# Gated recurrence and gated causal unit: GpSimd's square, addition and product as one operation per chunk of 1024 tokens, under a newly written order of all queues

## Chip, cores, metric

The kernel runs on one core of a Trainium2 chip. The metric is the time of one execution on the device in microseconds (us). Three runs of the kernel before took 288.52, 288.65 and 288.95 us; the median is 288.65 us.

## What is computed

Four sequences of 6336 tokens with 256 channels, 25344 tokens in all. First a gated linear recurrence, then a gated unit with a causal convolution of five taps:

```python
sig_r, sig_i = sigmoid(r_gate), sigmoid(i_gate)
a = exp(8 * sig_r * log(sigmoid(a_param)))
u = sqrt(max(1 - a*a, 1e-6)) * sig_i * x
for t in range(S): h = a[:, t] * h + u[:, t]; y[:, t] = h      # h = 0 at t = 0
gate = sigmoid(sum_k conv_w[k] * y[:, t - 4 + k])              # zeros ahead of t = 0
out = (gate * (y @ w_val)) @ w_out
```

Inputs and output are float32. The kernel keeps most intermediate tiles in bfloat16.

## The kernel before

**Tiling.** The tokens are cut into 51 windows (w0 to w50): w0, w1 and the last have 256 tokens, all others 512. Windows are joined to 28 chunks (line 17): chunks 0 to 2 and 26, 27 hold one window, chunks 3 to 25 two, so chunk c holds w(2c-3) and w(2c-2), 1024 tokens. The 256 channels are two halves h of 128 partitions.

**Stations of a chunk.** Each word of the string ORDER (line 38) is one step, a two-letter name with its numbers, and behind @ the PSUM banks that it writes. The string is played word by word (line 557), each step issuing its instructions on one engine; so ORDER fixes the order within every engine's queue. Between engines only semaphores order the work. An engine never passes a waiting instruction.

- lr, li, lx (window): loads of r, i, x, 512 KB each, on SyncE's queue (L292), into rings of four windows each. A load waits until its place was read for the last time.
- ta, tb (chunk): ScalarE's tanh of half of r (L310) and of i (L313). They free the places of r and i.
- pp (window, L320): GpSimd adds one to the tanh of i, in place. up (window, L332): GpSimd multiplies it with x and writes u, freeing the place of x. For windows 1, 2 and 6 uv does both on VectorE (L346), from a copy of x that TensorE makes (xp, L337).
- tr (chunk, h): TensorE transposes the tanh of r, for one chunk or for a pair (GROUPS, line 35; L357). ex (chunk, h): ScalarE's exponential gives a (L378).
- sq (chunk, h, L386): GpSimd squares a into the ring of squares. In two places ScalarE does it (sa.25.1 and sa.27.1, L394).
- rt (batch, L405): ScalarE's square root of 1 - a*a for a batch of mostly three chunks (BATCHES, line 20; rt.10 is chunks 23 to 25, rt.11 is 26 and 27). The square root needs another activation table, so a table is loaded ahead of nearly every rt and another behind it (L562).
- nt (chunk): TensorE transposes the roots (L420); xg: VectorE multiplies them with u (L450); xt: TensorE transposes back (L461); sc (chunk, h): VectorE's scan, the recurrence itself (L483). For chunks 26 and 27 u is transposed first and the product follows (L435, L446).
- cv (window): TensorE's convolution with 20 matmuls (L495). tg: ScalarE's tanh of it (L502), into a ring of three. vl: y @ w_val (L510). gv: VectorE's product (L515). ou: the last product (L525). cd or ca: copy to SBUF by VectorE (L533) or ScalarE (L535). st: store on SyncE's queue (L546).
- wm: five matmuls whose result nobody reads (L364).

**What orders the work around the change.** GpSimd's queue holds only sq, pp, up and four casts at the start. A chunk of 1024 tokens takes six instructions there: two sq, two pp, two up, each over 128x1024 elements. rt of a batch waits for all squares of the batch, xg of a chunk for its u, and lx of a later window for up of the window that held its place.

Places in the rings: r and i use place (w + 1) mod 4, so that the two windows of a chunk stand side by side; x uses w mod 4, by which w3 (place 3) and w4 (place 0) do not.

Of the kernel before, what the change touches and what calls it, by code (L numbers as in the profile page):

```python
# [9 lines left out]
P = 128  # L10
# [3 lines left out]
ACT = mybir.ActivationFunctionType  # L14
# [3 lines left out]
    [512, 512], [512, 512], [512, 512], [512, 512], [512, 512], [512, 512], [512, 512], [512, 512], [512, 512],  # L18
    [512, 512], [512, 512], [512, 512], [512, 512], [512, 512], [512, 512], [512, 512], [512], [256]]
BATCHES = [[0], [1], [2], [3, 4], [5, 6, 7], [8, 9, 10], [11, 12, 13], [14, 15, 16], [17, 18, 19], [20, 21, 22],  # L20
    [23, 24, 25], [26, 27]]
# [17 lines left out]
s_ident s_small s_kt s_diag lr.2 lr.0 s_wl.3 lr.1 li.0 lr.3 s_wl.2 ta.2 ta.0 lr.4 tr.0.1@0 tr.2.0@1 lr.6 ta.1 lr.5  # L39
tr.1.0@2 tb.0 tr.0.0@3 li.1 tr.2.1@4 ex.2.0 li.2 tr.1.1@5 li.3 ex.1.1 lx.0 ex.0.1 sq.1.1 li.4 ex.1.0 sq.2.0 ex.0.0  # L40
ex.2.1 sq.1.0 ta.3 sq.2.1 pp.0 sq.0.0 sq.0.1 ta.4 tb.1 lr.10 tr.3.0@4,5 tb.2 lr.9 lr.8 lr.7 lx.2 tr.3.1@2,3 ex.3.0
s_wl.1 up.0 lx.1 lx.4 wm.10@6 ex.3.1 sq.3.0 wm.5@6 lx.3 wm.3@6 tb.3 sq.3.1 wm.9@6 wm.6@6 ta.6 pp.4 sq.4.1 ta.5 lr.13
li.5 xp.2@2,3 li.6 sq.4.0 li.7 lr.14 tr.5.0@4,5 lx.6 uv.2 pp.3 rt.0 rt.2 nt.0@0 up.4 xg.0 rt.1 xt.0@0,1 xp.1@2 rt.3
sc.0.0 nt.1@3 up.3 lx.5 nt.2@0 uv.1 s_wl.0 xg.1 xg.2 xt.1@2,3 sc.0.1 lx.7 sc.1.0 nt.3@6,7 lr.12 sc.1.1 xg.3 ex.5.0
xt.2@0,1 sc.2.1 sc.2.0 tb.4 cv.0@2,3 tr.5.1@4,5 xt.3@6,7 lr.11 li.8 sq.5.0 ex.5.1 tg.0 sc.3.0 pp.5 sc.3.1 cv.2@0,1
s_wcast cv.1@4,5 ta.8 xp.6@2,3 uv.6 vl.0@6,7 tg.1 tg.2 vl.2@0,1 up.5 ta.7 sq.6.1 lx.8 li.9 li.10 lr.17 lr.18
nt.4@2,3 gv.0 tb.5 tr.7.0@6,7 ou.0.0@4 gv.2 ex.7.0 xg.4 sq.6.0 cd.0.0 tr.7.1@0,1 sq.5.1 vl.1@2,3 ou.2.0@4,5 ex.7.1
gv.1 xt.4@6,7 ou.1.0@2 lx.9 li.12 cv.4@0,1 cd.2.0 cv.3@4,5 pp.7 sq.7.1 tb.6 pp.8 sq.7.0 tg.4 tg.3 rt.4 sc.4.1 st.0
sc.4.0 li.11 lr.15 lr.16 st.2 up.7 pp.9 li.14 li.13 vl.3@0,1 vl.4@4,5 gv.3 gv.4 cd.1.0 ou.3.0@0,1 pp.10 up.8 sq.8.1
cd.3.0 cv.6@6,7 st.1 ou.4.0@2,3 wm.12@4 tg.6 cd.4.0 wm.1@4 nt.5@2,3 xg.5 lx.10 tb.7 st.3 vl.6@0,1 gv.6 ta.9 xt.5@2,3  # L50
ou.6.0@0,1 cv.5@6,7 nt.6@4,5 ta.10 up.9 sc.5.0 sc.5.1 lx.11 up.10 wm.0@2 tr.9.0@2,3 tg.5 st.4 lx.12 tb.8 vl.5@6,7
ex.9.0 xg.6 cd.6.0 xt.6@4,5 pp.11 sq.8.0 pp.12 tr.9.1@0,1 up.11 ex.9.1 li.16 li.15 lr.19 lr.20 gv.5 lr.22 st.6 lr.21
nt.7@6,7 cv.7@2,3 sc.6.1 up.12 ou.5.0@0,1 sc.6.0 sq.9.0 tg.7 tb.9 cv.8@2,3 cd.5.0 xg.7 lx.13 lx.14 li.18 ta.11
vl.7@4,5 cv.9@0,1 xt.7@6,7 gv.7 tr.11.1@4 tg.9 tg.8 ex.11.1 ta.12 ou.7.0@0,1 st.5 lx.15 lx.16 li.17 li.19 lr.26
lr.24 sc.7.1 sc.7.0 cv.10@2,3 vl.10@4,5 wm.7@7 vl.8@6,7 tg.10 sq.10.1 pp.13 pp.14 sq.10.0 cd.7.0 sq.9.1 pp.15 gv.10
rt.5 gv.8 st.7 lr.23 li.20 vl.9@2,3 up.13 up.14 tr.12.0@0 pp.16 ou.10.0@4,5 gv.9 ou.8.0@6,7 cd.8.0 ou.9.0@2,3
wm.16@1 nt.8@6,7 tr.11.0@1 cd.9.0 cd.10.0 tb.10 sq.11.1 up.16 xg.8 cv.11@4,5 lx.17 st.9 lr.25 xt.8@6,7 sc.8.1 tg.11
vl.11@2,3 wm.17@4 ex.12.0 tr.12.1@0 nt.9@4,5 gv.11 pp.17 up.15 pp.18 ex.11.0 ex.12.1 sq.12.1 sq.11.0 cv.12@2,3
sq.12.0 xg.9 ta.13 wm.13@7 ou.11.0@4,5 sc.8.0 xt.9@0,1 cd.11.0 cv.14@6,7 cv.13@4,5 tb.11 tg.12 ta.14 tg.14 tg.13
tr.13.0@2,3 tr.13.1@6,7 sc.9.0 ex.13.0 sc.9.1 up.17 st.10 li.21 vl.12@4,5 ex.13.1 nt.10@0,1 lx.18 li.22 gv.12 up.18  # L60
xg.10 lr.28 st.8 lr.27 tb.12 vl.13@2,3 st.11 ou.12.0@4,5 xt.10@0,1 cv.16@6,7 pp.20 pp.19 sq.13.1 gv.13 ou.13.0@2,3
lx.20 lx.21 lr.30 lx.19 ta.15 sq.13.0 pp.21 up.20 cd.12.0 cv.15@4,5 sc.10.1 sc.10.0 lr.29 li.23 tg.16 cd.13.0 li.24
lx.22 tg.15 vl.16@6,7 vl.14@4,5 gv.14 cv.18@0,1 vl.15@2,3 pp.22 rt.6 up.19 li.25 ou.14.0@4,5 gv.16 gv.15 cd.14.0
wm.14@6 ou.15.0@2,3 tg.18 lr.31 li.26 nt.11@4,5 sq.14.0 sq.14.1 up.21 up.22 vl.18@6,7 cd.15.0 xg.11 xt.11@4,5 tb.13
gv.18 cv.17@0,1 nt.12@6,7 ta.16 lr.32 lx.23 sc.11.1 lx.24 st.15 pp.23 pp.24 xg.12 st.13 li.27 li.28 vl.17@2,3
tr.15.1@6,7 sc.11.0 tg.17 tb.14 up.23 ou.16.0@0,1 cd.16.0 ex.15.1 ta.17 cv.19@4,5 lr.34 lr.33 tg.19 gv.17 xt.12@0,1
tr.15.0@6,7 st.14 lx.25 sc.12.0 sc.12.1 li.30 ou.17.0@2,3 pp.25 ex.15.0 ou.18.0@4,5 cv.20@6,7 up.24 tb.15 cd.17.0
cd.18.0 tg.20 cv.21@0,1 pp.26 sq.15.1 sq.16.1 nt.13@2,3 vl.19@6,7 tg.21 xg.13 st.12 lx.26 lx.28 st.17 lx.27 sq.15.0
li.29 st.16 li.31 lr.35 gv.19 vl.20@0,1 gv.20 xt.13@2,3 ou.20.0@0,1 sc.13.0 sq.16.0 vl.21@6,7 ou.19.0@4,5 gv.21
ta.18 cd.20.0 sc.13.1 ou.21.0@6,7 cv.22@0,1 lr.38 st.20 lr.36 rt.7 ca.19.0 li.32 lr.37 up.25 pp.27 up.26 pp.28 lx.29  # L70
nt.14@4,5 cd.21.0 xg.14 vl.22@2,3 tr.17.1@6,7 tg.22 tb.16 up.28 up.27 ex.17.1 nt.15@0,1 lx.30 gv.22 xg.15 xt.14@4,5
tr.17.0@2,3 cv.23@0,1 sc.14.0 sc.14.1 ex.17.0 pp.30 cv.24@6,7 pp.29 st.19 tg.23 vl.24@2,3 ou.22.0@0,1 tg.24 gv.24
vl.23@6,7 xt.15@4,5 ta.19 sq.18.1 sq.18.0 sq.17.0 sq.17.1 ou.24.0@2,3 tb.17 cd.22.0 gv.23 li.33 li.34 cv.26@0,1
up.29 cd.24.0 ou.23.0@6,7 st.18 ta.20 pp.32 ca.23.0 tg.26 cv.25@2,3 up.30 pp.31 sc.15.0 tg.25 li.35 tr.19.0@6,7
nt.16@0,1 vl.25@2,3 sc.15.1 xg.16 st.21 cv.27@4,5 ex.19.0 gv.25 lx.31 lx.33 xt.16@0,1 st.22 lx.32 lx.34 tr.19.1@6,7
lr.40 li.36 lr.39 st.23 tb.18 sc.16.0 sc.16.1 ou.25.0@2,3 tg.27 sq.19.0 ex.19.1 cv.28@4,5 tg.28 pp.34 sq.20.0
vl.28@6,7 vl.26@4,5 sq.19.1 lr.42 lr.41 cd.25.0 gv.28 wm.19@0 vl.27@2,3 gv.26 up.31 ou.28.0@6,7 up.32 up.34 pp.33
# [29 lines left out]
def kernel(  # L107
# [82 lines left out]
    with tc.manual_schedule():  # L190
# [403 lines left out]
```

## Time and profile before

| | |
|---|---|
| runs | 288.52, 288.65, 288.95 us |
| span of the profiled execution, first to last instruction | 286.4 us |
| from that span to the median of the runs | 2.25 us |
| ScalarE (ACT) busy | 273.6 us, 198 instructions |
| TensorE (PE) busy | 251.8 us |
| VectorE (DVE) busy | 246.8 us |
| GpSimd (POOL) busy | 241.6 us, 161 instructions |
| moved by DMA | 104.76 MB, mean 366 GB/s |

The profiled execution's own time is known by its span only; what lies around the span is taken as the 2.25 us to the median. The page of the profile names busy time by engine, then 40 slices of the span with the busy share in tenths (9 is 90% or more), and the groups of instructions with their mean duration. The view by form keeps shapes apart; the waits say which engine stood still for whom; the timeline and the chain of waits give start and length in us. Instructions of one engine overlap a little at their ends, so the step from one start to the next is shorter than a duration, and busy time by windows joins the overlaps.

### The profile page before, as it was taken

What the parts mean: (1) busy time and instruction counts of PE and PEld (TensorE: products, weight loads), DVE (VectorE), ACT (ScalarE), POOL (GpSimd) and SP (SyncE); (2) the same over time, 40 slices, a digit from 0 to 9 for tenths busy, and PEclk for the clock granted to TensorE, in tenths of its full rate; (3) what the DMA queues carried; (4) which work ended last, traced back from release to release, by engine and by line L of the source; (5) the groups of instructions that cost most, each with busy time, mean ns of one, the idle gap of its engine ahead of it and who ended that gap; (6) DMA issues with size and microseconds to landing.
All of it is one profiled execution on the core that took longest, in us unless ns stands there. A gap on an engine that the chain in (4) does not pass through costs nothing.

```text
span 286.4 us, 6382 instructions
## 1 busy us (share of the span) xinstructions
PE 251.8 (88%) x2552; PEld 171.1 (60%) x2576; DVE 246.8 (86%) x214; ACT 273.6 (96%) x198; POOL 241.6 (84%) x161
## 2 busy tenths in 40 slices
PE   1387778899999999988988999989989899999993
PEld 1253447456656767455756676656646774767562
DVE  4002898969999899999999999999999999999991
ACT  5999999999999999999999999999999999898984
POOL 1659589899999999999999999999996999874600
PEclk9999999999999999999999999999999999999999
DMA  7999999999999999999999999999999999994536
GB/s 243 384 373 407 409 403 408 388 366 376 410 408 366 418 367 392 414 410 334 405 364 413 411 332 356 420 416 419 415 401 333 359 416 406 364 356 170 192 150 256
DMA packets 29996, 104.76 MB, mean 366 GB/s; under 512 B 3335, under 2 KB 3854, under 8 KB 29966
## 3 DMA queue, kind: packets, MB, share of 16 engines
q1 hardware_dynamic: 29952, 104.35, 94.5%
q8 instruction: 20, 0.33, 0.5%
q14 instruction: 10, 0.08, 0.1%
q10 hardware_dynamic: 14, 0.01, 0.0%
HBM read 78.39 MB, written 25.95 MB: 364 GB/s over the span
## 4 chain that ended last, share of the span: by engine, by line
ACT 33%; PE 29%; DVE 14%; issue 12%; DMA 8%; SPq 1%; ACTq 0%; DVEq 0%
ACT ering L405 8%; PE banks L495 8%; DVE yring L483 7%; PE banks L525 7%; DMA rring<-in_r_gate_dram 6%; ACT tgring L502 6%; ACT taring L310 5%; ACT tbring L313 5%; ACT aring L378 5%; PE banks L510 5%; PE banks L461 3%; DVE tgring L515 3%; PE banks L420 3%; ACT L562 3%; DVE oring L533 2%
## 5 line engine op out<-in xcount | busy, mean ns | idle before, releaser
L386 POOL TENSOR_TENSOR ering<-aring 128x1024 f32<-128x1024 f32 (+2 forms) x54 | 91.5, 1714 | 16.7 <-ACT aring L378 16.4
L332 POOL TENSOR_TENSOR uring<-tbring,xring 128x1024 bf16<-128x1024 bf16 (+1 forms) x48 | 101.1, 2119 | 3.6 <-DMA xring<-in_x_dram 3.1
L483 DVE TENSOR_TENSOR_SCAN yring<-aring,yring,banks 128x1024 bf16<-128x1024 f32 (+5 forms) x50 | 101.7, 2064 | 2.1 <-PE banks L461 1.9
L495 PE MATMUL banks<-yring,diag 64*64 64x512 bf16 (+7 forms) x1080 | 62.1, 361 | 2.3 <-ACT aring L378 1.6
L515 DVE SCALAR_TENSOR_TENSOR tgring<-tgring,banks 128x1024 bf16<-128x1024 bf16 (+1 forms) x51 | 59.1, 1178 | 4.0 <-PE banks L510 3.4
L320 POOL TENSOR_SCALAR tbring<-tbring 128x1024 bf16<-128x1024 bf16 (+1 forms) x48 | 49.1, 1032 | 6.8 <-ACT tbring L313 6.7
L378 ACT ACTIVATE aring<-banks,khf 128x2048 f32<-128x2048 bf16 (+3 forms) x38 | 54.2, 1476 | 0.4 <-PE banks L357 0.3
L525 PE MATMUL banks<-wo,tgring 128*128 128x256 bf16 x396 | 51.0, 274 | 3.7 <-DVE tgring L515 3.2
L502 ACT ACTIVATE tgring<-banks 128x1024 bf16<-128x1024 f32 (+1 forms) x51 | 50.2, 1011 | 2.0 <-PE banks L495 1.9
L510 PE MATMUL banks<-yring,wv 128*128 128x512 bf16 (+4 forms) x192 | 48.1, 359 | 3.7 <-ACT tgring L502 1.9
L310 ACT ACTIVATE taring<-rring 128x2048 bf16<-128x2048 f32 (+2 forms) x28 | 47.9, 1718 | 1.4 <-DMA rring<-in_r_gate_dram 1.4
L525 PEld LDWEIGHTS <-tgring 128*128 128x128 bf16 x396 | 41.2, 114 | 13.1 <-DVE tgring L515 8.8
L313 ACT ACTIVATE tbring<-iring 128x2048 bf16<-128x2048 f32 (+2 forms) x28 | 48.2, 1726 | 0.0
L405 ACT ACTIVATE ering<-ering 128x4096 bf16<-128x4096 f32 (+5 forms) x16 | 44.8, 2840 | 0.1
L495 PEld LDWEIGHTS <-diag 64*64 64x64 bf16 x1080 | 29.0, 106 | 25.6 <-issue 9.9
L533 DVE COPY oring<-banks 128x1024 f32<-128x1024 f32 (+1 forms) x36 | 41.9, 1182 | 1.4 <-PE banks L525 0.7
L357 PE MATMUL banks<-ident_b,taring 128*128 128x128 bf16 x396 | 29.9, 230 | 9.4 <-ACT taring L310 6.7
L357 PEld LDWEIGHTS <-taring 128*128 128x128 bf16 x396 | 26.5, 103 | 14.2 <-ACT taring L310 7.4
L510 PEld LDWEIGHTS <-wv 128*128 128x128 bf16 x216 | 19.7, 98 | 24.5 <-issue 10.3
L450 DVE TENSOR_TENSOR uring<-banks,uring 128x2048 bf16<-128x2048 bf16 (+2 forms) x26 | 29.4, 1134 | 3.5 <-PE banks L420 3.2
L420 PE MATMUL banks<-ident,ering 128*128 128x128 f32 x192 | 28.3, 289 | 1.1 <-ACT ering L405 0.9
L461 PE MATMUL banks<-ident,uring 128*128 128x128 f32 x192 | 25.9, 276 | 3.5 <-DVE uring L450 2.8
(49 smaller groups left out, 154.0 us busy)
## 6 DMA issues: line engine op xcount, KB each, us to landing
rring<-in_r_gate_dram SPq DMA_DIRECT2D x48, 512.0 KB, 8.2
iring<-in_i_gate_dram SPq DMA_DIRECT2D x48, 512.0 KB, 8.7
xring<-in_x_dram SPq DMA_DIRECT2D x48, 512.0 KB, 8.2
out_dram<-oring SPq DMA_DIRECT2D x48, 512.0 KB, 6.5
rring<-in_r_gate_dram SPq DMA_DIRECT2D x3, 256.0 KB, 4.1
iring<-in_i_gate_dram SPq DMA_DIRECT2D x3, 256.0 KB, 6.5
xring<-in_x_dram SPq DMA_DIRECT2D x3, 256.0 KB, 8.5
out_dram<-oring SPq DMA_DIRECT2D x3, 256.0 KB, 5.2
```

What stands on the lines that cost most here:

```text
L310: nc.scalar.activation(**tangent(c, taring, NTR, rring, NRI))
L313: nc.scalar.activation(**tangent(c, tbring, NTI, iring, NII))
L332: nc.gpsimd.tensor_tensor(out=u, in0=t1, in1=xt, op=ALU.mult)
L378: nc.scalar.activation(out=dst, in_=src, func=ACT.Exp, scale=khf[:, h:h + 1], bias=khf[:, h:h + 1])
L386: nc.gpsimd.tensor_tensor(out=e, in0=a, in1=a, op=ALU.mult)
L405: nc.scalar.activation(out=ering[:].bitcast(BF16)[:, 4 * o:4 * o + 2 * n], in_=ering[:, 2 * o:2 * o + 2 * n], func=ACT.Sqrt, scale=-0.25, ...
L483: nc.vector.tensor_tensor_scan(out=yring[:, h, col:col + o1 - o0], data0=aring[:, h, a_at[c] + o0:a_at[c] + o1], data1=xT[:, o0:o1], initi ...
L495: nc.tensor.matmul(out=gp[oh * 64:oh * 64 + 64, h, a:b], lhsT=diag[half * 64:half * 64 + 64, h, k, :], rhs=yring[half * 64:half * 64 + 64, ...
L502: nc.scalar.activation(out=tgring[:, w % NTG, :, 0:wins[w]], in_=live.pop(("gp", w))[:, :, 0:wins[w]], func=ACT.Tanh, scale=0.5)
L510: nc.tensor.matmul(out=val[:, m, a:b], lhsT=wv[:, hk, m * P:(m + 1) * P], rhs=yring[:, hk, col:col + b - a], start=(hk == 0), stop=(hk == ...
L515: nc.vector.scalar_tensor_tensor(out=tgring[:, w % NTG, :, 0:wins[w]], in0=tgring[:, w % NTG, :, 0:wins[w]], scalar=1.0, in1=live.pop(("va ...
L525: nc.tensor.matmul(out=ops[:, j * D:(j + 1) * D], lhsT=gv[:, hk, j:wins[w]:J], rhs=wo[:, hk, :], start=(hk == 0), stop=(hk == H - 1))
```

## The change

GpSimd gets one instruction per two-window chunk for each of its three jobs: sq.c squares both halves at once (2048 elements per partition), pc.c adds one for both windows, uc.c multiplies both windows with x. The new functions, and the place of x, which now is that of r and i:

```diff
-                dst = xring[:, w % NX, 0:J, :]
+                dst = xring[:, place(w, NX), 0:J, :]
...
+        def op_pc(c):
+            w, k = cwins[c][0], len(cwins[c])
+            t = tbring[:, place(w, NTI):place(w, NTI) + k, 0:wins[w] // P, :].rearrange("p w j d -> p (w j d)")
+            nc.gpsimd.tensor_scalar(out=t, in0=t, scalar1=1.0, scalar2=1.0, op0=ALU.mult, op1=ALU.add)
...
+        def op_uc(c):
+            w, k = cwins[c][0], len(cwins[c])
+            t, x, u = place(w, NTI), place(w, NX), (w + 1) % NU
+            nc.gpsimd.tensor_tensor(out=uring[:, u:u + k].rearrange("p w q d two -> p (w q) two d"),
+                                    in0=tbring[:, t:t + k].rearrange("p w (q two) d -> p (w q) two d", two=2),
+                                    in1=xring[:, x:x + k].rearrange("p w (q two) d -> p (w q) two d", two=2), op=ALU.mult)
...
+        def both_squares(c):
+            n = clen[c]
+            return (ering[:, H * e_at[c]:H * (e_at[c] + n)].rearrange("p (h n) -> p h n", h=H),
+                    aring[:, :, a_at[c]:a_at[c] + n])
+
+        def op_sq(c, *h):
+            e, a = squares(c, h[0]) if h else both_squares(c)
             nc.gpsimd.tensor_tensor(out=e, in0=a, in1=a, op=ALU.mult)
```

ORDER is written anew from the first to the last word, with other banks. Counted word by word: sq 54 -> 33 (23 of them over both halves), sa 2 -> 0, pp 48 -> 4 and pc 0 -> 22, up 48 -> 4 and uc 0 -> 22, cd 36 -> 35, ca 15 -> 16, wm 17 -> 11. Chunks 0 to 2, 26 and 27, and chunk 4, of which VectorE does w6, keep the smaller operations. Table loads stay at 18 in the loop; all other counts are equal. Parts of the new order to which the prediction refers:

```text
loads, start    before: lr.2 lr.0 s_wl.3 lr.1 li.0 lr.3 s_wl.2 lr.4 lr.6 lr.5 ...   after: lr.0 lr.2 lr.1 lr.3 lr.4 lr.6 lr.5 li.0 lx.0 ...
ScalarE, start  before: ta.2 ta.0 ta.1 tb.0 ex.2.0 ...    after: ta.0 ta.2 ta.1 ex.2.1 ex.1.1 ...
ScalarE, after  tb.4 tg.2 ex.7.0 ex.7.1 tb.5 tg.4 tb.6 tg.3 rt.4 tg.5 tb.7 ta.10 ta.9 tg.6 tb.8 ex.9.0 ex.9.1 ta.12
                rt.6 tg.16 ta.16 ta.15 tg.17 tg.18 tb.14 ex.15.0 ex.15.1 ta.18 ta.17 tb.15 tb.16
                ex.23.1 ta.25 ca.34 tb.23 ex.25.0 tg.38 ex.25.1 tg.37 tb.24 tg.39 rt.10
GpSimd, after   pc.21 uc.21 pc.22 uc.22 sq.24 sq.23 sq.25 pc.23 uc.23 pc.24 uc.24 pc.25 uc.25 sq.26.1 pp.49 ...
TensorE, end    before: cv.41 vl.37 ou.38 cv.40 ou.37 nt.23 vl.41 vl.40 nt.24 xt.23 ou.39 cv.42 ou.41 ... cv.45 cv.46 vl.45 vl.46 xt.26 cv.48 cv.47 xt.27 ou.46 ou.45 ...
                after:  cv.40 ou.37 nt.23 vl.40 ou.38 xt.23 ou.39 cv.42 cv.41 ... xt.27 xt.26 ou.44 ou.43 cv.47 cv.48 cv.46 vl.47 ou.45 vl.46 ...
```

More of the change, by code (lines that the diff above doesn't have):

```diff
@@ L44 @@
[L44 to L53, printed above, removed]
@@ L103 @@
+ca.49.0 st.49 vl.50@6,7 gv.50 ou.50.0@6 ca.50.0 st.50
 """
@@ L249, in s_kt, with s_diag @@
                                     scalar2=4.0 * math.log(1.0 - 1e-6), op0=ALU.max, op1=ALU.min)
-        def s_diag():
-            wps = banks[:, 1]
+        def s_diag(at):
+            wps = banks[:, at]
             for h in range(H):
@@ L327, in u_args @@
             return (uring[:, (w + 1) % NU, 0:wins[w] // (2 * P)].rearrange("p q d two -> p q two d"),
-                    by_pair(tbring[:, place(w, NTI)], w), by_pair(xring[:, w % NX], w))
+                    by_pair(tbring[:, place(w, NTI)], w), by_pair(xring[:, place(w, NX)], w))
         def op_up(w):
@@ L337, in op_xp @@
                 nc.tensor.matmul(out=ps[:, q], lhsT=ident[:],
-                                 rhs=xring[:, w % NX, 2 * q:2 * q + 2, :].rearrange("p two d -> p (two d)"),
+                                 rhs=xring[:, place(w, NX), 2 * q:2 * q + 2, :].rearrange("p two d -> p (two d)"),
                                  start=True, stop=True)
```

135 lines of the change are left out of this document (65 added, 70 removed).

## The prediction

> **What bounds the kernel now.** I read the page's busy time and its 40 slices first, then the waits, then the timeline around the last big square root.
>
> ```profile
> PE 251.8 (88%) x2552; PEld 171.1 (60%) x2576; DVE 246.8 (86%) x214; ACT 273.6 (96%) x198; POOL 241.6 (84%) x161
> ACT  5999999999999999999999999999999999898984
> POOL 1659589899999999999999999999996999874600
> DMA  7999999999999999999999999999999999994536
> ```
>
> ScalarE is at 9 from the second slice to the 34th, and so are GpSimd, nearly, and the DMA engines. Which of them is the limit is told by who waits for whom.
>
> ```profile
> ACT oring L535 <- PE banks L525: 2.8, 4, 1.1
> ACT tgring L502 <- PE banks L495: 1.9, 3, 1.1
> ACT taring L310 <- DMA rring<-in_r_gate_dram: 1.4, 4, 0.5
> 220.00:240.00 20.00, 18.65 (x232) 13.01 (x227) 19.42 (x14) 19.96 (x16) 19.84 (x13) 1.00 1.01 387
> 240.00:250.00 10.00, 9.61 (x78) 6.96 (x78) 9.68 (x9) 9.21 (x5) 8.87 (x6) 1.00 0.99 373
> 250.00:260.00 10.00, 9.95 (x107) 6.49 (x108) 10.00 (x8) 8.35 (x11) 6.66 (x5) 1.00 0.96 345
> 265.00:270.00 5.00, 4.95 (x67) 2.50 (x64) 5.00 (x4) 4.97 (x6) 4.24 (x4) 1.00 0.72 270
> ```
>
> The first three rows are ScalarE's waits: total, times, longest. It never waits for GpSimd. The windows (columns: PE, PEld, DVE, ACT, POOL, clock, DMA share, GB/s) show two stages. Up to 245 us ScalarE is busy 19.96 of 20 us: its own list of work is the limit. From 245 us ScalarE falls to 8.35 of 10 and TensorE and VectorE are at 9.95 and 10.00: there they set the pace. The border is the end of rt.10:
>
> ```profile
> 237.57 1.28 ACT L562 ACT_TABLE_LOAD   x1
> 238.87 5.33 ACT L405 ACTIVATE ering<-ering 128x6144 bf16<-128x6144 f32 x1
> 244.25 1.23 PE L420 MATMUL banks<-ident,ering 128*128 128x128 f32 x8
> 282.82 0.58 ACT L535 COPY oring<-banks 128x512 f32<-128x512 f32 x1 [0.88 <-PE banks L525]
> ```
>
> rt.10 ends at 244.20 us; nt.23 starts 0.05 us later, and from there to the end of the span pass 42.2 us.
>
> **GpSimd's operations.** The view by form gives each job at two sizes.
>
> ```profile
> L332 POOL TENSOR_TENSOR uring<-tbring,xring 128x1024 bf16<-128x1024 bf16 x46 | 98.7, 2161 | 0.3
> L386 POOL TENSOR_TENSOR ering<-aring 128x1024 f32<-128x1024 f32 x45 | 84.4, 1896 | 6.1 <-ACT aring L378 5.8
> L320 POOL TENSOR_SCALAR tbring<-tbring 128x1024 bf16<-128x1024 bf16 x46 | 47.8, 1050 | 6.8 <-ACT tbring L313 6.7
> L386 POOL TENSOR_TENSOR ering<-aring 128x512 f32<-128x512 f32 x4 | 4.2, 1039 | 2.9 <-ACT aring L378 2.9
> L332 POOL TENSOR_TENSOR uring<-tbring,xring 128x512 bf16<-128x512 bf16 x2 | 2.3, 1166 | 3.3 <-DMA xring<-in_x_dram 3.1 <-POOL tbring L320 0.2
> L320 POOL TENSOR_SCALAR tbring<-tbring 128x512 bf16<-128x512 bf16 x2 | 1.2, 619 | 0.0
> L394 ACT ACTIVATE ering<-aring 128x1024 f32<-128x1024 f32 x1 | 1.1, 1122 | 0.0
> ```
>
> A square of 1024 costs 1896 ns, of 512 1039 ns: 857 ns for 512 elements, so 1896 - 2x857 = 182 ns are paid once per instruction. Likewise the product 2x1166 - 2161 = 171 ns, the addition 2x619 - 1050 = 188 ns. No row is longer than 1024. If the line goes on, 2048 cost 3.61, 4.15 and 1.91 us; the nearest bound above is twice 1024, 3.79, 4.32 and 2.10 us; a still higher price is a rival below. I take the line: 23 x 0.182 + 22 x 0.171 + 22 x 0.188 = 12.1 us saved. GpSimd takes over the two squares of ScalarE, 1.9 us for 1024 elements and 0.6 us for 256 by the line: net 9.6 us less of 241.6. On the path: nothing. ScalarE does not wait for GpSimd, and between 60 and 240 us ScalarE is the limit. What the merging costs is delay: a square starts only when both halves of a are there, and the place of the first x is freed with the second's. I cost these at nothing: ahead of rt.10, for instance, the new order leaves after ex.23.1 nine ScalarE steps and a table load, about 12.5 us by the steps below (an exponential of one chunk taken as 1.1), and GpSimd needs 3 x 3.6 = 10.8 us for sq.24, sq.23, sq.25. That cover, 1.7 us, is lost if GpSimd comes late by more; then ScalarE waits for the rest, at each of seven batches.
>
> **ScalarE's list.** These rows give the steps from start to start: tanh of a chunk 1.80, of a window 0.90, each 0.1 below the duration.
>
> ```profile
> 213.09 1.90 ACT L310 ACTIVATE taring<-rring 128x2048 bf16<-128x2048 f32 x1
> 214.89 1.01 ACT L502 ACTIVATE tgring<-banks 128x1024 bf16<-128x1024 f32 x1
> 215.79 1.91 ACT L313 ACTIVATE tbring<-iring 128x2048 bf16<-128x2048 f32 x1
> 171.21 2.10 ACT L378 ACTIVATE aring<-banks,khf 128x2048 f32<-128x2048 bf16 x1
> 173.16 1.96 ACT L313 ACTIVATE tbring<-iring 128x2048 bf16<-128x2048 f32 x1
> ```
>
> (An exponential of two chunks: 1.95.) Ahead of rt.10 both orders hold the same words of ScalarE except sa.25.1, three copies each. Its 1.12 us are a step of 1.0, so rt.10 can come **1.0 us** earlier. The square sa.27.1 and the copy that is added fall behind rt.10, where ScalarE has idle time: nothing.
>
> **The start.**
>
> ```profile
> 4.54 1.58 ACT L310 ACTIVATE taring<-rring 128x1024 bf16<-128x1024 f32 x2 [0.49 <-DMA rring<-in_r_gate_dram]
> 24.55 1.91 ACT L310 ACTIVATE taring<-rring 128x2048 bf16<-128x2048 f32 x1 [0.28 <-DMA rring<-in_r_gate_dram]
> 26.48 1.28 ACT L562 ACT_TABLE_LOAD   x1
> ```
>
> The first tanh waits 0.49 us for 512 KB of r. Now the half-sized lr.0 comes first. But the last tanh ahead of the table load (24.55) also waits for r, and both orders must by then have loaded the same windows of r and i: the DMA engines set this date. I take **-0.4 us**, between 0 and -1.5 (all ScalarE waits of the start gone).
>
> **The loads' turn.** A place of r or i is loaded again after its tanh, and the queue needs this long from issue to landing (minimum, median, maximum for r, then for i):
>
> ```profile
> DMA to landing us min/median/max: 3.8/8.0/11.1
> DMA to landing us min/median/max: 4.1/8.6/10.2
> L292 SPq DMA_DIRECT2D iring<-in_i_gate_dram x51: 327/430/1416, 2.9 to 247.3; - x51
> ```
>
> The second load of a chunk is issued 0.4 us after the first, so a chunk's turn takes about 9.0 us for i and 8.4 us for r. In the order before, the shortest turn of i that I count by steps is 11.1 us, and of r, after the start, 9.2 us. The new order has four short ones. tb.4 to tb.6: 0.9 + 3.9 + 1.8 + 0.9 = 7.5 us, so a wait of 1.5 us. ta.10 to ta.12: 1.8 + 0.9 + 1.8 + 3.9 = 8.4 us, just enough. ta.16 to ta.18 with 9.3 and tb.14 to tb.16 with 9.3 are enough. Behind a waiting tb.6 stand tg.3 and rt.4 and all that follows on ScalarE, and every us there is a us of the end. I take **+1.5 us**; with all landings at their minimum it is 0, with all at their maximum 3.1 + 3.1 + 2.2 + 1.3 = 9.7 us.
>
> **The end.** TensorE takes its words in order, so what stands behind nt.23 cannot be done ahead of rt.10's end. Before, these were the convolutions of w42 to w50 and the last products of w39 to w50; after, cv.41 and ou.38 stand there too. Their prices are on the chain of waits (start, length), that of a copy in the view by form:
>
> ```profile
> 255.37 1.21 PE banks L495 x20
> 262.86 1.75 PE banks L525 x16
> L533 DVE COPY oring<-banks 128x1024 f32<-128x1024 f32 x34 | 40.6, 1212 | 1.4 <-PE banks L525 0.7 <-issue 0.4
> ```
>
> 1.21 + 0.87 (half of 1.75) = 2.1 us. VectorE has a copy more there too (cd.47, 1.2 us). TensorE's idle time from 240 to 280 us is about 0.6 us (9.61 and 9.95 of 10 above, then 4.95 or more of each 5), so I take **+1.5 us**: the new work first fills what is idle. The other end is 2.1 + 1.2 = 3.3 us, with the copy on top. TensorE's six fewer bursts of unread matmuls (wm) save nothing: none lay in this stretch before.
>
> **Sum.** 286.4 - 1.0 - 0.4 + 1.5 + 1.5 = 288.0 us of span. The profiled execution is known by its span; the median of the runs, 288.65, lies 2.25 us above it, so the forecast is **290.3 us**, 0.6% slower.
>
> **Rivals.**
>
> *ScalarE's shorter list reaches the end.* Ahead of rt.11 the new order has one window's tanh (0.9) and sa.27.1 (256 elements, about 0.3) less than before, beyond the 1.0 and the 0.4. If the last section simply hangs on rt.11, the span ends 286.4 - 2.6 = 283.8, and with the 1.5 us of the loads 285.3: 287.6 us, faster; without the loads' wait 286.1. For it: ScalarE still shows waits for TensorE only of 2.8 and 1.9 us. Against it: behind xt.26 the new order puts ou.44, ou.43, cv.46 and vl.46 that stood ahead of it before, 3.8 us of TensorE. It decides whether TensorE has nothing left to do when rt.11 ends.
>
> *The terms cancel.* Landings at 7.5 us instead of 9.0 take the 1.5 us away: span 286.5, 288.75 us.
>
> *ScalarE waits for TensorE and VectorE in the middle.* VectorE was busy 19.42 of 20 us; where a tg of the new order comes ahead of its convolution, ScalarE stands. A wait of 0.5 us per window tanh on ten windows would give 5 us: 295 us. For it: every engine is near 95%. Against: the order before shows only 1.9 us of such waits.
>
> *Merging does not pay, or costs.* Bound: at twice 1024 GpSimd needs 10.2 us for a chunk, and ScalarE passes a chunk in about 10.1 us (18 chunks from 55.3 to 237.6 us), so GpSimd at worst is as tight as before, and time stays as forecast. A price above this makes GpSimd the limit: at 10.5 us per chunk it would add 18 x 0.4 = 7.2 us, 297.5 us.
>
> ```profile
> 55.32 1.28 ACT L562
> ```
>
> The Trainium skill speaks for this rival: its page "GPSIMD Engine Reference", section 3.1, gives 4497 ns for an addition of two tensors of 2048 float32. By that figure a square would cost 0.9 us more than on my line, a chunk 10.6 us, and the kernel would come out around 299 us. The trace does not agree at half the size: 1896 ns for 1024 is 1.85 ns per element, the page's is 2.20.
>
> *TensorE's clock falls* where wm is missing. In the trace it held at 1.00 over an idle stretch of 4.49 us:
>
> ```profile
> 13.08 1.03 PE L357 MATMUL banks<-ident_b,taring 128*128 128x128 bf16 x8 [4.49 <-ACT taring L310]
> 10.00:15.00 5.00, 1.03 (x8) 0.77 (x8) 0.00 (x0) 4.62 (x5) 4.18 (x6) 1.00 1.02 397
> ```
>
> The Trainium skill ("TensorE: Matmul & The Clock Gate", part 1) has the clock halve after about 3.4 us without work; this row speaks against that. By rows alone: 2.5 us of TensorE's work behind rt.10 taking twice as long would give 292.8 us.
>
> **How the numbers follow.** Forecast case, slower by 0.2 to 1.3%: 0.48. ScalarE's list reaches the end: 0.20, faster. Terms cancel: 0.17, no change. Waits in the middle: 0.09. GpSimd dearer: 0.04. Clock: 0.02. So faster 0.20, same 0.17, slower 0.63; 0.2%, about 0.6 us, is what a measurement of this kernel can tell from no change. The range runs from 287.4, a little below the faster case with its wait, to 293.2, which takes in the end term at its upper bound and two long landings: outside are about 0.08 below and 0.11 above.
>
> **What would show it.** Right: GpSimd's rows at 2048 elements near 3.6, 4.15 and 1.9 us and its busy time near 232 us; rt.10 ending near 244 us; a wait of ScalarE's tb.6 or ta.12 for a load; more than 43 us from nt.23 to the end. Wrong: no wait of tb and ta for loads; ScalarE waiting for GpSimd ahead of an rt; under 42.2 us behind rt.10; ScalarE below 19.9 of 20 us in the middle for waits on TensorE or VectorE.

## The result: 304.28 us, 5.6% slower

The kernel after takes 304.28 us (median of 4 runs, 303.01 to 305.75) against 288.58 us for the kernel before beside it: 1.056 times as long, 95% interval 1.0522 to 1.0599. The prediction of 290.3 us had the sign right and missed the size: 15.7 us were lost, not 1.7, and the time lies far outside its range of 287.4 to 293.2.

The page of the profile after (span 302.5 us):

```profile
PE 254.9 (84%) x2546; PEld 169.8 (56%) x2546; DVE 246.7 (82%) x213; ACT 274.3 (91%) x197; POOL 234.5 (78%) x96
ACT  6999999899999969799899999999999579989853
PEclk9995999999999997999999999999999959999998
```

Every engine does nearly the work it did before (TensorE 3 us more, GpSimd 7 us less); what grew is idle time on all of them. ScalarE's row, an unbroken line of nines up to slice 34 before, has deep dents in slices 15, 17, 32 and 33 and shallow ones in 8 and 20; TensorE's clock, at 9 all along before, has dents of its own in slices 4, 16 and 33, and a shallow one in the last. ScalarE's waits (total, times, longest) say for whom it stood:

```profile
ACT aring L384 <- POOL ering L397: 5.9, 2, 3.1
ACT tgring L505 <- PE banks L498: 4.3, 6, 2.1
ACT tbring L307 <- DMA iring<-in_i_gate_dram: 1.6, 2, 1.3
ACT tbring L307 <- POOL ering L397: 1.4, 1, 1.4
ACT ering L408 <- POOL ering L397: 1.0, 1, 1.0
```

The first row is new in kind: before, ScalarE never waited for GpSimd. An exponential (L384) writes a, a square (L397) reads it, so the exponential waits until the square is done. The timeline shows the two places, ScalarE first, then GpSimd:

```profile
112.94 2.06 ACT L384 ACTIVATE aring<-banks,khf 128x2048 f32<-128x2048 bf16 x1 [2.81 <-POOL ering L397]
241.60 1.20 ACT L384 ACTIVATE aring<-banks,khf 128x1024 f32<-128x1024 bf16 x1 [3.10 <-POOL ering L397]
249.59 1.02 ACT L505 ACTIVATE tgring<-banks 128x1024 bf16<-128x1024 f32 x1 [2.06 <-PE banks L498]
257.27 1.28 ACT L565 ACT_TABLE_LOAD   x1
```

```profile
109.30 3.60 POOL L397 TENSOR_TENSOR ering<-aring 128x2048 f32<-128x2048 f32 x1 [2.24 <-ACT aring L384]
234.41 7.15 POOL L397 TENSOR_TENSOR ering<-aring 128x2048 f32<-128x2048 f32 x2
```

ex.13.1 starts at 112.94, when sq.11 ends (109.30 + 3.60); ex.25.0 starts at 241.60, when sq.23 ends (234.41 + 7.15). Yet neither writes what that square reads. In the built program the merged square reads a in two runs, one for each half, 5120 elements apart, and the semaphores treat it as if it read all that lies between (call this stretch its reach; e14 below tests it); ex.13.1 writes there. A square of one half reads one run, so it holds up only what writes that run.

Behind both stalls comes a third loss. TensorE, which had waited for ScalarE, fell to half speed:

```profile
115.05 1.05 PE L363 MATMUL banks<-ident_b,taring 128*128 128x128 bf16 x16 [2.97 <-ACT aring L384]
115.94 1.66 PE L528 MATMUL banks<-wo,tgring 128*128 128x256 bf16 x8
243.77 1.86 PE L528 MATMUL banks<-wo,tgring 128*128 128x256 bf16 x8 [3.43 <-ACT tgring L505]
247.27 2.26 PE L498 MATMUL banks<-yring,diag 64*64 64x512 bf16 x20
240.00:250.00 10.00, 6.57 (x44) 2.96 (x37) 4.76 (x4) 6.34 (x6) 6.67 (x3) 0.66 0.45 173
```

After 2.97 us of idle time the transposes still ran in their usual 1.05 us, but the last product of a window behind them took 1.66. After 3.43 us such a product took 1.86 us and a convolution 2.26, where the kernel before shows 1.04 to 1.07 and 1.27; the granted clock of these 10 us was 0.66. The tanh of that convolution is the third row of ScalarE's timeline above: it waited 2.06 us.

Last, the stretch behind rt.10, as one window each, after and before (the columns are as in the prediction's windows):

```profile
257.26:302.50 45.24, 39.75 (x410) 27.07 (x410) 36.78 (x30) 35.10 (x37) 17.50 (x11) 0.98 0.56 216
```

```profile
244.20:286.40 42.20, 37.30 (x377) 25.55 (x382) 35.11 (x29) 34.13 (x37) 17.84 (x13) 0.99 0.66 245
```

It is 3.0 us longer. Where the 16.1 us of span went: end +3.0; exponentials behind squares +5.9; rt behind squares +1.0; tanh behind TensorE +3.9 (2.06 behind the second fall of the clock; 1.10 at 121.65 us, likely behind the first, as TensorE worked without a gap from 115.05 us until then; 0.32 and 0.40); tanh of i behind loads +3.0 (1.45, 0.32, 1.28); the start 0.6 and sa.25.1 1.0 us less. That adds up to 15.2; the other 0.9 us lie in shorter gaps. (For the 1.45 us of tb.6 the view names GpSimd's square, which ended at 54.21 us, just ahead of tb.6 at 54.26; but tb.6 uses nothing of that square. The load of its place was issued at about 46.0 us and took some 8.3 us to land, and e5 below names it.)

### The profile page after: what moved, and what is told of

Read it like the earlier page. It is cut to its first block, busy times and chain, and to the rows that moved or that the text cites. A ratio compares the mean times of both kernels' runs of the same rounds, so it can differ in the third digit from the quotient of the medians.

```text
span 302.5 us, 6260 instructions
## 1 busy us (share of the span) xinstructions
PE 254.9 (84%) x2546; PEld 169.8 (56%) x2546; DVE 246.7 (82%) x213; ACT 274.3 (91%) x197; POOL 234.5 (78%) x96
## 5 line engine op out<-in xcount | busy, mean ns | idle before, releaser
L397 POOL TENSOR_TENSOR ering<-aring 128x2048 f32<-128x2048 f32 (+2 forms) x33 | 90.3, 2751 | 30.1 <-ACT aring L384 28.8
L336 POOL TENSOR_TENSOR uring<-tbring,xring 128x2048 bf16<-128x2048 bf16 x22 | 90.7, 4125 | 7.7 <-DMA xring<-in_x_dram 6.6
L498 PE MATMUL banks<-yring,diag 64*64 64x512 bf16 (+7 forms) x1080 | 63.8, 366 | 4.2 <-ACT tgring L505 1.0
L384 ACT ACTIVATE aring<-banks,khf 128x2048 f32<-128x2048 bf16 (+3 forms) x38 | 54.5, 1468 | 6.2 <-POOL ering L397 5.9
L528 PE MATMUL banks<-wo,tgring 128*128 128x256 bf16 x396 | 52.5, 279 | 8.2 <-ACT tgring L505 5.0
L513 PE MATMUL banks<-yring,wv 128*128 128x512 bf16 (+4 forms) x216 | 51.0, 371 | 4.8 <-ACT tgring L505 3.1
L536 DVE COPY oring<-banks 128x1024 f32<-128x1024 f32 (+1 forms) x35 | 40.6, 1184 | 7.4 <-PE banks L528 3.7
L320 POOL TENSOR_SCALAR tbring<-tbring 128x2048 bf16<-128x2048 bf16 x22 | 41.9, 1905 | 5.6 <-ACT tbring L307 5.6
L363 PE MATMUL banks<-ident_b,taring 128*128 128x128 bf16 x396 | 27.8, 223 | 9.9 <-ACT taring L304 3.6
L423 PEld LDWEIGHTS banks<-ident,ering 128*128 128x128 f32 x192 | 25.4, 209 | 14.1 <-ACT ering L408 4.2
L363 PEld LDWEIGHTS <-taring 128*128 128x128 bf16 x396 | 24.4, 99 | 15.1 <-issue 9.9
```

Source lines behind the costliest of these rows:

```text
L336: nc.gpsimd.tensor_tensor(out=uring[:, u:u + k].rearrange("p w q d two -> p (w q) two d"), in0=tbring[:, t:t + k].rearrange("p w (q two) d ...
L363: nc.tensor.transpose(out=bank[:, o:o + P], in_=taring[:, place(w, NTR), j, h * P:(h + 1) * P], identity=ident_b[:])
L384: nc.scalar.activation(out=dst, in_=src, func=ACT.Exp, scale=khf[:, h:h + 1], bias=khf[:, h:h + 1])
L397: nc.gpsimd.tensor_tensor(out=e, in0=a, in1=a, op=ALU.mult)
L423: nc.tensor.transpose(out=bank[:, k:k + P], in_=ering[:, e + q:e + wins[w] // 2:nq], identity=ident[:])
L498: nc.tensor.matmul(out=gp[oh * 64:oh * 64 + 64, h, a:b], lhsT=diag[half * 64:half * 64 + 64, h, k, :], rhs=yring[half * 64:half * 64 + 64, ...
```

## The experiments

Times are medians; each ratio, and what is said to be lost or won back, is against the kernel before that ran beside it (287.8 to 288.1 us; 288.6 for the kernel after).

**e1_halves.** The kernel after, squares by halves again at the same places.

```diff
-            e, a = squares(c, h[0]) if h else both_squares(c)
-            nc.gpsimd.tensor_tensor(out=e, in0=a, in1=a, op=ALU.mult)
+            for k in h or range(H):
+                e, a = squares(c, k)
+                nc.gpsimd.tensor_tensor(out=e, in0=a, in1=a, op=ALU.mult)
```

> The changed kernel with each merged square issued as two instructions, one per half, at the same place of the queue (56 squares for 33); the additions and products stay merged, the order stays new. Theory A (spans): the merged square reads a in two runs 5120 elements apart; the waits of the built program take it for everything between the first and the last element, so ScalarE's exponentials of other chunks wait for it (in the changed profile 2.8 us at 110 and 3.1 us at 238 us, and behind them the waits of tanh for TensorE and the halved clock). By it the exponentials' waits for squares go, and the time falls from 304.3 to 290 to 294 us, what is left being the wait of tb.6 (1.5 us) and the longer end (1.5 to 3 us). Theory B (order): the new order itself loses the time; then it stays above 300 us. Theory C (long operations release late, whatever the addresses): 292 to 300 us.

296.11 us, 1.0275 (1.0237 to 1.0312). The waits of exponentials for squares are gone. The merged squares are half of the loss, 7.7 of 15.7 us; the other 8.0 us have another cause.

**e2_side_by_side.** The kernel after, but the two halves of a chunk's a lie next to each other, so the merged square reads one run.

```diff
-        aring = rings.tile([P, H, NA], FP32, name="aring")
+        aring = rings.tile([P, H * NA], FP32, name="aring")
...
-                    aring[:, :, a_at[c]:a_at[c] + n])
+                    aring[:, H * a_at[c]:H * (a_at[c] + n)])
```

> The changed kernel with the same instructions in the same order, squares merged; only a lies otherwise in its ring: the two halves of a chunk side by side, so that the merged square reads one run of 2048. Theory A (spans): no exponential waits for a square any more, 290 to 294 us, within 1 us of the kernel with halves. Theory B (order): above 300 us. Theory C (long operations release late): above 300 us, since the operations are as long as before.

301.0 us, 1.0471 (1.042 to 1.0522). Only a part came back, and the waits of VectorE and ScalarE show why this was no clean test:

```profile
DVE yring L485 <- ACT aring L384: 2.9, 1, 2.9
ACT aring L384 <- PE banks L363: 2.7, 2, 2.4
```

Now an exponential of two chunks writes two runs, and a scan of the half that lies between them waits for it, 2.9 us in one place; TensorE, which waits for the scan, then held up ScalarE for 2.4. The long reach had moved from the squares to the exponentials.

**e3_old_order_merged_squares.** The kernel before, squares of chunks 3 to 24 merged at the place of the second half, a as it was.

```diff
         def op_sq(c, h):
+            if len(cwins[c]) == 2 and c != 25:
+                if c not in seen:
+                    seen.add(c)
+                    return
+                e, a = both_squares(c)
```

> The kernel before with its old order, additions and products by window; only the squares of chunks 3 to 24 are merged, each at the place of its second half, a in the old layout of two runs. In the built program four exponentials then wait for a square of another chunk. Theory A (spans): slower than before by 2 to 8 us (290.5 to 296.5). Theory B (order): 288 to 289 us, as before. Theory C: 289 to 292 us.

305.85 us, 1.0613 (1.0584 to 1.0642): merged squares alone, in the old order, lose as much as the whole change, dearer than any theory said.

```profile
ACT tbring L313 <- POOL uring L332: 6.7, 2, 6.1
POOL ering L398 <- ACT aring L378: 32.1, 10, 7.6
ACT aring L378 <- POOL ering L398: 1.9, 2, 1.5
```

GpSimd waited 32.1 us for exponentials (16.4 before). A merged square must wait for both halves, products queue behind it, and ScalarE's tanh of i, which needs the place that a product frees, stood 6.1 us behind one. Exponentials stood behind squares for only 1.9 us: in this order the squares cost mostly by being late, not by their reach.

**e4_old_order_all_merged.** The kernel before with squares (a side by side as in e2), additions and products merged at the later place, x one place on.

```diff
+            last = second("up", w)
+            if last is False:
+                return
+            if last:
+                return op_uc(chunk_of[w])
```

> The kernel before with its old order, and all three jobs merged, each at the place of the later of its two instructions, a's halves side by side, x one place on; the two squares on ScalarE stay there. Theory A (spans): no exponential waits for a square, GpSimd is 10 us lighter but not the limit: 287.5 to 289.5 us. Theory B (order): the same. Theory C (long operations release late): 291 to 296 us, since the place of the first x and the first half's square come 2 us later.

294.66 us, 1.0237 (1.0209 to 1.0265), where theory A said no change.

```profile
DVE uring L493 <- POOL uring L362: 5.0, 5, 2.8
ACT aring L410 <- DVE yring L526: 1.4, 1, 1.4
```

VectorE waits for u, and an exponential waits for a scan as e2's layout makes possible; neither wait is in the kernel before. So lateness costs as well, or the reach of the exponentials, and this run doesn't part the two.

**e5_new_order_alone.** As e1, with additions and products by windows too: what is left is the order, and x one place on.

```diff
         def op_uc(c):
-            w, k = cwins[c][0], len(cwins[c])
...
+            for w in cwins[c]:
+                op_up(w)
```

> The kernel after, with every merged instruction taken apart again at its place: squares by halves of a, additions and products by windows. What is left of the change is the order of the queues and x one place on. The run with only the squares taken apart (e1_halves) took 296.1 us. Theory P (the merged products free u and the places of x late, and GpSimd is late ahead of the square roots by them, 1.25 and 0.50 us of waits seen in e1_halves): the rest of the loss goes with them, 290 to 293 us. Theory O (the new order itself costs the rest: three tb that wait 1.64, 1.58 and 0.30 us for loads, and 45.3 us behind rt.10 against 42.2): 294.5 to 297 us.

296.89 us, 1.0304 (1.0265 to 1.0344): theory O. The order alone costs 9 us, and merging the products on top nothing (e1 against e5). ScalarE's waits, and the stretch behind rt.10:

```profile
ACT tbring L307 <- DMA iring<-in_i_gate_dram: 4.2, 4, 2.0
ACT taring L304 <- DMA rring<-in_r_gate_dram: 2.2, 3, 0.9
248.78:295.30 46.52, 39.62 (x405) 27.27 (x410) 36.48 (x30) 35.21 (x37) 20.69 (x17) 0.99 0.58 231
```

From the table load ahead of rt.0 (26.49, as before) to the end of rt.10 it is 4.6 us slower: waits for loads of 2.03, 0.35, 0.34, 0.90 and 1.51 us, less the 1.0 of sa.25.1, make 4.1 of it. The end is 4.3 us longer.

**e6_two_squares_halved.** The kernel after with two of its 23 merged squares by halves.

```diff
+            if c in (11, 23):
+                h = range(H)
```

> The kernel after, with only the squares of chunks 11 and 23 by halves; 21 squares stay merged. Theory S (the merged squares cost only where an exponential of ScalarE really stood behind one of them, sq.11 at 110 us and sq.23 at 238 us, and by the clock that fell behind these two): nearly all that e1_halves won comes back with 2 of 23, 296 to 298.5 us. Theory L (each merged square costs a little, by its late end): about 2/23 of 8.2 us comes back, 302.5 to 304.5 us.

298.31 us, 1.0377 (1.0344 to 1.041): theory S. Two squares bring back 5.2 of the 7.7 us of e1. Where ex.13.1 had waited 2.81 us it now follows the tanh ahead of it at once:

```profile
111.84 2.10 ACT L384 ACTIVATE aring<-banks,khf 128x2048 f32<-128x2048 bf16 x1
```

**e7_old_order_merged_products.** The kernel before; additions and products merged as in e4, squares untouched.

> The kernel before in its own order, with the additions and products of a chunk merged at the place of the later one and x one place on; the squares stay by halves. With the squares merged too (e4_old_order_all_merged) it took 294.7 us. Theory P (the late products cost): 291 to 295 us, with waits of VectorE for u and of GpSimd for x. Rival (the squares were the cost in that run too): 288 to 289.5 us.

289.5 us, 1.0056 (1.0037 to 1.0076), at the rival's upper edge: late products cost 1.6 us, so most of e4's loss of 6.6 us is its squares. VectorE's wait for u, absent before, is small:

```profile
DVE uring L482 <- POOL uring L362: 3.6, 3, 2.0
```

**e8_square_off_scalare.** The kernel before, one word of ORDER.

```diff
-sa.25.1
+sq.25.1
```

> The kernel before with one word changed: the square of chunk 25's second half is done by GpSimd in place of ScalarE. The prediction's first term (ScalarE's list up to rt.10 is the limit, each step off it is time off the end): 1.0 us less, 286.9 to 287.4 us. Rival (GpSimd's 1.9 us more come ahead of rt.10, or TensorE and VectorE set the end, so nothing comes of it): 287.9 to 289 us.

288.68 us, 1.0037 (1.0022 to 1.0052): slower, not 1.0 us faster.

```profile
235.61 1.02 ACT L502 ACTIVATE tgring<-banks 128x1024 bf16<-128x1024 f32 x1 [0.96 <-PE banks L525]
DVE uring L450 <- POOL uring L332: 1.2, 2, 0.7
```

The microsecond taken off ScalarE came back as a wait of 0.96 us for TensorE in front of rt.10, and GpSimd's additional square made u late for VectorE behind it, a wait that the kernel before does not show.

**e9_end_alone.** The kernel before, with cv.41, tg.41, ou.38 and cd.38 moved behind nt.23.

```diff
-gv.39 cv.41@0,1 st.33 ... ou.38.0@2,3 gv.37 li.47 rt.10 cv.40@4,5 tg.41 ou.37.0@6,7 cd.38.0 nt.23@2,3
+gv.39 st.33 ... gv.37 li.47 rt.10 cv.40@4,5 ou.37.0@6,7 nt.23@2,3 ... cv.41@0,1 tg.41 xg.23 ou.38.0@2,3 cd.38.0
```

> The kernel before with the end term alone: the convolution of w41 and the last product of w38 (with its copy by VectorE) stand behind nt.23 as in the kernel after, everything else in the old order. The prediction's term (the moved work first fills what is idle): 1.5 us more than before, 289.0 to 289.6 us. Rival (it comes on top in full, 2.1 us of TensorE and up to 1.2 us of the copy, as the tails of the new order seem to say with 39.75 us of TensorE's work against 37.30 and no less idle time): 289.7 to 291.5 us. If it is hidden: under 288.5 us.

292.17 us, 1.0143 (1.0117 to 1.0169). In this kernel the product of w38 reads the gate's place after tg.41 has written it, and so uses w41's gate and waits for its tanh, a detour that the kernel after doesn't have. The time is not used; e13 does it again without.

**e10_order_loads_spared.** e5 with three repairs of the order.

```diff
-tb.6 cv.3@0,1 tg.3 pc.5 pc.6 uc.5 ... rt.4 tg.5
+cv.3@0,1 tg.3 pc.5 uc.5 ... rt.4 tb.6 pc.6 tg.5
...
-lr.21 lr.22 li.16 lr.20 li.18 li.15
+li.15 lr.21 lr.22 li.16 lr.20 li.18
...
-tb.16 tg.20 ... rt.7 vl.20@6,7
+tg.20 ... rt.7 tb.16 vl.20@6,7
```

> The new order alone (e5_new_order_alone, 296.9 us) with three repairs at the places where a tanh of i waited for its load: tb.6 and tb.16 (with their additions) go behind rt.4 and rt.7, where nothing needs them yet, and the load of w15 goes ahead of those in SyncE's queue that wait for a later tanh. Theory R (these waits, 2.03, 1.51 and 0.35 us, are the loss up to rt.10): 292.5 to 294 us, rt.10 about 3.9 us earlier. Rival (ScalarE's waits move to what is late next, TensorE or the next load): 295.5 to 297 us.

303.83 us, 1.0538 (1.0498 to 1.0578): 7 us worse than without the repairs. The timelines of SyncE and of ScalarE:

```profile
51.73 12.92 SPq L286 DMA_DIRECT2D iring<-in_i_gate_dram  x3
```

```profile
74.73 4.01 ACT L380 ACTIVATE aring<-banks,khf 128x2048 f32<-128x2048 bf16 x2 [1.89 <-PE banks L359]
80.93 1.91 ACT L304 ACTIVATE taring<-rring 128x2048 bf16<-128x2048 f32 x1 [2.19 <-DMA rring<-in_r_gate_dram]
```

The loads that refill tb.6's places stood in SyncE's queue from 51.73 us until the tanh, now behind rt.4, was done: a group of three took 12.92 us (4.74 in e5), and everything queued behind it came late. I had moved the tanh and forgotten whom its place feeds.

**e11_merged_products_loads_spared.** The same repairs in e1.

> The same three repairs in the kernel with merged additions and products and the squares by halves (e1_halves, 296.1 us): what is left of the change once the merged squares are taken apart and the loads are spared. Theory R: 292 to 293.5 us. Rival (waits move on): 295 to 296.5 us. None expects it under the kernel before.

304.07 us, 1.0544 (1.0486 to 1.0601): 8 us worse than e1, as e10 is than e5.

**e12_additions_merged.** The kernel before with 20 merged additions.

```diff
+            if len(cwins[c]) == 2 and c not in (4, 18, 20):
+                if c not in half:
+                    half.add(c)
+                    return
```

> The kernel before with one part of the change alone that delays nothing: 20 of the additions of one merged at the place of the later one (chunks 18 and 20 stay apart, where a product stands between). Some 3.8 us less of GpSimd's work. Theory of the prediction (GpSimd is not on the path, saved time there is worth nothing): 287.5 to 288.6 us. Rival (GpSimd's list is a limit with ScalarE's, so what it saves shows): 284 to 287.2 us. A delay by the wait for the later tanh: over 288.8 us.

288.35 us, 1.0015 (0.9996 to 1.0035): no change, with 3.0 us less work on GpSimd (238.6 against 241.6). Time saved on GpSimd is worth nothing here, as predicted.

**e13_end_alone_own_places.** e9 again, with places that force no detour.

```diff
+nt.23@2,3 ... cd.37.0 tg.40 vl.40@0,1 xg.23 ou.38.0@6,7 gv.40 cv.41@4,5 tg.41 cd.38.0 vl.41@6,7
```

> The kernel before with the end term alone, done again: in e9_end_alone the tanh of w41 came ahead of the last product of w38, which lies in the same place of the gate's ring of three, so that product used w41's tanh and waited for it. Here the product of w38 (banks 6 and 7) and the convolution of w41 (banks 4 and 5) both stand behind nt.23, in the order of the kernel after. The prediction's term (the moved work first fills idle time): 1.5 us more than before, 289.0 to 289.8 us. Rival (in full on top, 2.1 us of TensorE and up to 1.2 us of the copy): 289.9 to 291.5 us. Hidden: under 288.5 us.

291.16 us, 1.0129 (1.0099 to 1.0159): 3.3 us, the rival's size. Up to rt.10 its timeline is that of the kernel before within 0.05 us, and the rest is this window:

```profile
244.20:289.60 45.40, 39.70 (x410) 26.85 (x410) 36.49 (x30) 34.28 (x38) 17.85 (x13) 0.97 0.61 226
```

TensorE's work in it is that of the kernel after (39.75 us), its length too (45.24). This move alone is enough for the longer end.

**e14_exponentials_swapped.** The kernel after, all 23 squares merged, ex.13.0 and ex.13.1 exchanged, ex.25.0 and ex.25.1 too.

```diff
-tg.13 sq.11 uc.11 ex.13.1 ... ex.13.0
+tg.13 sq.11 uc.11 ex.13.0 ... ex.13.1
```

> The kernel after with all 23 merged squares and only this changed: the two exponentials of chunks 13 and 14, and the two of chunk 25, change places with each other, so that the half of a which lies outside the reach of sq.11, or of sq.23, is written first. Theory A (reach: a square that reads two runs holds up what is written between them): the stall at sq.11 goes whole and most of that at sq.23, with the clock's fall behind them, 297.5 to 301 us. Theory C (the squares cost because one of 3.6 us ends later than one of 1.9): nothing changes, 302.5 to 305 us.

300.25 us, 1.0437 (1.0381 to 1.0493), below the kernel after's interval: theory A holds, for the two stalls.

```profile
111.24 2.06 ACT L384 ACTIVATE aring<-banks,khf 128x2048 f32<-128x2048 bf16 x1 [0.37 <-DVE yring L486]
124.86 5.33 ACT L408 ACTIVATE ering<-ering 128x6144 bf16<-128x6144 f32 x1 [2.08 <-POOL ering L397]
241.71 1.20 ACT L384 ACTIVATE aring<-banks,khf 128x1024 f32<-128x1024 bf16 x1 [1.07 <-POOL ering L397]
```

2.81 us of wait became 0.37 (for a scan) and 3.10 became 1.07, with nothing but the half exchanged. This wins 3.3 us. But a square root now waits 2.08 us for the last square of its batch, where the kernel after shows 0.97: part of the squares' cost is plain lateness.

**e15_new_order_without_i and e16_old_order_without_i.** e5 and the kernel before, each without the loads of i for w7 to w48.

```diff
         def op_li(w):
-            load(w, "i")
+            if w < 7 or w > 48:
+                load(w, "i")
```

> The new order alone (e5_new_order_alone, 296.9 us) without the loads of i for w7 to w48: the tanh takes what is left in the ring, so the values are others, and a fifth of the DMA traffic and the waits of SyncE's queue for tb are gone as well. Theory R (the order costs by its waits for loads, 4.2 us for i and 0.9 us for r, and by its end): 291 to 293 us, 3 to 5 us over the old order treated alike (next run). Rival (the waits move on to TensorE and VectorE, whose order is the cost): 295 us or more, 7 to 9 us over it.

> The kernel before without the loads of i for w7 to w48, the control for the run above: ScalarE never waited for i here, so both theories expect 286.5 to 288.5 us.

294.4 us, 1.0232 (1.0204 to 1.0261), and 287.88 us, 1.0006 (0.9991 to 1.002). Between the two theories: 6.5 us are left of 9.1. 4.2 us of waits for i went, 2.5 us of time came back, because others took their place:

```profile
119.73 5.33 ACT L406 ACTIVATE ering<-ering 128x6144 bf16<-128x6144 f32 x1 [0.63 <-POOL ering L395]
151.20 5.33 ACT L406 ACTIVATE ering<-ering 128x6144 bf16<-128x6144 f32 x1 [1.01 <-POOL ering L395]
164.48 4.01 ACT L381 ACTIVATE aring<-banks,khf 128x2048 f32<-128x2048 bf16 x2 [1.10 <-PE banks L360]
```

No version is faster than the kernel before.

## Why the prediction was wrong, point by point

**The step that failed** is this one: "What the merging costs is delay … I cost these at nothing", with its reason "ScalarE does not wait for GpSimd". The reason was a reading of the trace of before, where a square held up only the exponential that writes the same half five chunks later. The merged square holds up everything between its two runs, and the two runs are to be seen in the diff: aring[:, :, a:a+n], 5120 apart. Shown by e14 (two waits of 2.81 and 3.10 us fall to 0.37 and 1.07 with no square taken apart, 3.3 us won), with e1 (7.7 us back) and e6 (5.2 us with two squares). I looked for the delay where rt waits for squares and gave it a cover of 1.7 us at rt.10; that wait came to 1.0 us, at rt.6. The larger one stood elsewhere. This step is one half of the miss. The other half is the order: its terms (sa.25.1, start, loads, end) add up to 1.6 us and it cost 9.1 (e5); the paragraphs below say where they were short.

**GpSimd's prices** were right: forecast 3.61, 4.15 and 1.91 us, measured

```profile
L336 POOL TENSOR_TENSOR uring<-tbring,xring 128x2048 bf16<-128x2048 bf16 x22 | 90.7, 4125 | 7.7 <-DMA xring<-in_x_dram 6.6 <-DVE tgring L518 0.4
L397 POOL TENSOR_TENSOR ering<-aring 128x2048 f32<-128x2048 f32 x23 | 82.6, 3605 | 16.8 <-ACT aring L384 15.5 <-PE banks L423 1.2
L320 POOL TENSOR_SCALAR tbring<-tbring 128x2048 bf16<-128x2048 bf16 x22 | 41.9, 1905 | 5.6 <-ACT tbring L307 5.6
```

So the rival of a dearer GpSimd falls, and that nothing is won by its shorter list was right, as far as e12 shows it with the additions. Its busy time fell to 234.5 us, not to 232.

**sa.25.1, -1.0 us**: wrong in the old order. "its own list of work is the limit" holds only up to the next engine, and TensorE stood right behind ScalarE: 0.96 of the 1.0 us came back as a wait for it (e8). In e5 the account up to rt.10 (4.1 of 4.6 us) comes out with the 1.0 us taken off.

**The start, -0.4 us**: -0.6, but this may be luck: runs with the old start load the table ahead of rt.0 anywhere between 25.38 (e7) and 26.48 us (before).

**The loads' turn, +1.5 us**: right at the place named (tb.6 waited 1.45), too small in all. In e5 five such waits make 5.1 us. The turn of tb.16, 9.3 us, which I called enough, was not: it waited 1.51 us, because I took the median landing, while its load came about 11 us after its issue. And I did not follow SyncE's queue: li.15, for tb.9 (0.35 us), stood behind li.18, and lr.31, for ta.17 (0.90 us), behind a store and a load of x; neither turn is on my list. In e15 2.5 of 4.2 us of such waits came back as time, some 60%.

**The end, +1.5 us**: 3.0, and 3.3 alone (e13). The step "the new work first fills what is idle" failed: TensorE's 2.4 us came on top and its idle time grew, from 4.9 us of the 42.2 to 5.5 of the 45.2. The value lies at my upper bound, 3.3.

**From span to time, +2.25 us**: 1.9 (304.38 and 302.5 us in the profiled run).

**Waits in the middle**, given 0.09 at 5 us: a tanh behind TensorE waited 3.9 us ahead of rt.10, most of it after the stalls; in e5, without the merged squares, there is no such wait between 40 us and rt.10.

**The clock**, given 0.02: it did fall, twice right behind the stalls, and took 2.06 us of ScalarE's time, likely 3.2. The row that I held against it was misread: at 13.08 us eight transposes took 1.03 us, at 27.69 sixteen took 1.06.

```profile
27.69 1.06 PE L357 MATMUL banks<-ident_b,taring 128*128 128x128 bf16 x16
```

So TensorE did run at half speed after those 4.49 us, and the window's 1.00 for the clock at that place can't be right. The Trainium skill ("TensorE: Matmul & The Clock Gate", part 1) has the clock halve after an idle window of about 3.4 us and says that the window runs freely. The traces agree that the length of an idle time does not decide by itself: the clock fell after 3.43 us here and not after 3.33 in e1. They do not agree on a least length: it also fell after 2.97 us here and after 2.19 in e1.

Together: order 9.1 us (e5), merged squares 7.7 us (e1), merged products about nothing (e1 against e5; 1.6 us in the old order, e7). Not settled is how the squares' part divides between reach and lateness beyond the two stalls, since e2 and e4 brought a new reach with them, and what makes up the 2 to 3 us of the order that neither loads of i nor the end explain. The repairs of e10 and e11, meant to win back the waits for loads, brought new waits in their place.

## What to carry to other kernels

When two operations are merged into one, list whom the new one holds up: here it tied everything between its first and last element, and everything behind it in its queue waited for its latest input. A kernel whose engines have hardly any idle time has little cover: a wait removed from one engine came back from the next, whole in e8 and by some 40% in e15. So cost a moved step by all who wait for its inputs, its outputs and its places, and take the upper bound where the cover can't be named. Check a clock reading against two equal groups of instructions before it is used as evidence.

## What the runs showed of the hardware

- GpSimd's price is linear from 512 to 2048 elements: squares 1041, 1896 and 3605 ns, with about 0.18 us paid per instruction.
- TensorE's clock fell to half (granted clock 0.50) for some 3 to 7 us at a time: in the kernel after, by windows of 1 us, from about 116.2 to 119.6 us and from 242.5 to 249.3. The idle time ahead of it does not say by itself whether it falls. The same six matmuls at the start took 5.46 us after 3.73 us of idle time in the kernel after, 3.17 after 3.33 in e1:

```profile
24.68 5.46 PE L343 MATMUL banks<-xring,ident 128*128 128x512 f32 x6 [3.73 <-DMA xring<-in_x_dram]
```

```profile
24.65 3.17 PE L343 MATMUL banks<-xring,ident 128*128 128x512 f32 x6 [3.33 <-DMA xring<-in_x_dram]
```

But the sixteen transposes behind rt.6 took 3.49 us in e1 after only 2.19 us of idle time, with a granted clock of 0.50, and 2.19 us in the kernel after, after 1.68:

```profile
128.64 3.49 PE L424 MATMUL banks<-ident,ering 128*128 128x128 f32 x16 [2.19 <-ACT ering L409]
```

```profile
131.40 2.19 PE L423 MATMUL banks<-ident,ering 128*128 128x128 f32 x16 [1.68 <-ACT ering L408]
```
